# Moving two of the second block's four gate weight pieces behind the transposed gradient tiles in one DMA queue

## The chip, the cores and the metric

The kernel runs on one core of a Trainium2 chip. A core has a matrix engine (TensorE; PE for its matmuls and PEld for its weight loads in the profile), VectorE (DVE), ScalarE (ACT), GpSimd (POOL) and SyncE (SP), whose queue sends most of the DMAs. The metric is the device time of one execution in microseconds (us); lower is better.

## The reference, cut to what matters

The forward pass normalises x row by row and adds three terms; the kernel returns the output and the gradients of nine of its inputs.

```
xn   = layernorm(x)                                  # x: 2048 rows x 1024
out  = x + A(xn, k, v, shift_k, ssm_k, ssm_D)        # a long convolution branch
         + B(xn, W_gate, W_up, W_down)               # the gated branch:
gate = xn @ W_gate ; up = xn @ W_up                  # 1024 x 3584 each
h    = (gate if gate > 0 else 0) * up
B    = h @ W_down                                    # 3584 x 1024
# backward: gradients of out with respect to x, k, v, shift_k, ssm_k, ssm_D, W_gate, W_up, W_down
```

The backward pass of the gated branch needs `grad_out @ W_down.T`, the gradient of h.

## The kernel before, in words

Everything is bf16 with sums in float32. The change lies in the first phase, `hidden` (line 1221). It works in 14 blocks `n`: two halves of the rows (8 tiles of 128 rows each), and in each half seven blocks of 512 columns of the hidden dimension. For every row tile `s` of a block it makes three products of eight matmuls each (`gemm8`, line 1150): the gate, `ps_g`, from the transposed activation tile `xnT` and the gate weights `wg`; the up product, `ps_u`, from `xnT` and `wu`; and the gradient row, `ps_h`, from the transposed gradient tile `goT` and the transposed down weights `wdT`. Each of the three weight blocks comes in four pieces of 256 KB, piece q serving matmuls 2q and 2q+1 of a product. `col_block` (line 1136) sends the four pieces of the gate or up weights, `row_piece_T` (line 1168) one piece of the down weights, as a transposing DMA.

The first block (`n == 0`, `ahead` in the code) is special, since the layer norm runs at the same time. Activation tiles 0 to 5 are transposed on the matrix engine; tiles 6 and 7 by transposing DMAs in `flip_xn` (line 1185) that wait until VectorE has scaled these rows. Gradient tiles are transposed by DMA in `load_T` (line 1174). Its matmuls run in this order: rows 0 to 3 gate and up; gradient rows 0 and 1; gate and up of rows 4 and 5; gradient rows 2 to 5; gate and up of rows 6 and 7; gradient rows 6 and 7. Then the second block begins: gate of rows 0 and 1, up of rows 0 and 1, gradient rows 0 and 1, and so on.

The weights of the second block are loaded during the first: the gate weights by `load_gate` (line 1244) after gradient rows 0 and 1, into buffers that are spare; the up weights into the buffers of the first block's gate weights, and the down weights into those of its up weights, as these become free.

All these loads go through SP's queue, which issues in order: an entry that waits holds back all behind it. A scheduler sets the order of the entries from priorities that grow through the program; `issue_after(x)` keeps what is written under it behind `x`, and `pin` keeps an instruction in the written order. A DMA on SP's queue carries one of eight semaphores in turn and waits until the DMA eight places before it is complete. In this stretch the queue holds: four gate pieces of the second block, gradient tiles 4 and 5, activation tiles 6 and 7, gradient tiles 6 and 7, four up pieces, four down pieces. POOL's queue sends the stores of this block: `h_d`, `ug_d`, and the normalised rows `xn_d`.

Of the kernel before, what the change touches and what calls it, by code (L numbers as in the profile page):

```python
# [17 lines left out]
P = 128  # L18
# [30 lines left out]
class ABranch:  # L49
# [47 lines left out]
    def load(self, out, in_):  # L97
        self.pri.now()
        ins = self.nc.sync.dma_start(out=out, in_=in_)
        if self.pin:  # L100
            self.tc.keep_in_program_order(ins)
        else:
            self.pri.pin(ins)
# [776 lines left out]
class LnMlp:  # L880
# [252 lines left out]
            st0 += n  # L1133
            yield

    def col_block(self, W, fb, name, s, amid={}, ahead=None):

        out = []
        for q in range(self.DT // 2):
            if q in amid:  # L1140
                amid[q]()
            t = self.w_tile(name, 4 * s + q)
            first = ahead is not None and q == 0
            ins = (ahead if first else self.nc.sync).dma_start(
                out=t[:], in_=W[q * 256:(q + 1) * 256, fb * 512:(fb + 1) * 512].rearrange("(k p) f -> p k f", p=P))
            self.pri.pin(ins, always=first)
            out.append(t)
        return lambda kt: out[kt // 2][:, kt % 2, :]

    def gemm8(self, ps, xT, w, mid=None, after={}):  # L1150
# [22 lines left out]

    def load_T(self, src, st, name, slot, always=False):
        t = self.act_tile(name, slot)
        self.pri.pin(self.nc.sync.dma_start_transpose(out=t[:].rearrange("p (a b) -> p a b", b=P),
                                                      in_=src[st * P:(st + 1) * P, :]), always=always)
        return t

    def load_nat(self, src, st, name, slot):  # L1180
# [40 lines left out]
    def hidden(self, first, goT, load, ln, tables, Wg, Wu, Wd, g, xn_d, h_d, ug_d):  # L1221
# [6 lines left out]
        for n in range(N):  # L1228
            half, fb = divmod(n, self.FB)
            s0, cols, ahead = half * HS, slice(fb * 512, fb * 512 + 512), n == 0  # L1230
# [6 lines left out]
            wg, wu, wdt = w  # L1237
            wd = lambda kt, t=wdt: t[kt // 2][:, kt % 2, :]
            sg, su, sd = sets
            to = (spare, sg, su) if ahead else (sg, su, spare)  # L1240
            nb = (n + 1) % self.FB
            ru, nw, late = {}, [None, None, None], []

            def load_gate():
                if last:
                    self.slab_part(h_d, 0, "hs", self.hs, 4, sg)
                else:
                    nw[0] = self.col_block(Wg, nb, "wg", to[0])

# [4 lines left out]
            def load_down(q):  # L1254
                if last and q == 0:
                    self.slab_part(h_d, 0, "hs", self.hs, 0, spare)
                elif not last:
                    if q == 0:
                        nw[2] = []
                    nw[2].append(self.row_piece_T(Wd, nb, "wdT", to[2], q, n == 1))  # L1260
# [105 lines left out]
            def gate_up(sp):  # L1366
                end = sp == HS - 2
                if ahead and not end:
                    gate(sp)
                    yield from step(self.PACE[0])  # L1370

                    def turn():
                        flip(sp + 2)
                        with self.tc.issue_after(self.copied.ins):
                            chunk()
                    up(sp, None, {4: turn})
                    yield from step(self.PACE[1])
                    gate(sp + 1)
                    yield from step(self.PACE[0])
                    up(sp + 1)  # L1380
                    yield from step(self.PACE[1])
                    return
                rows = [(f, s) for f in (gate, up) for s in (sp, sp + 1)]
                for f, s in sorted(rows, key=lambda r: r[1]) if ahead else rows:
                    f(s)
                    yield from step(self.PACE[f is up])
                    if end and f is gate and s == sp + 1:
                        (load_up if ahead else load_gate)()
                if end and ahead:
                    for q in range(4):  # L1390
                        load_down(q)
                elif end:
                    load_up()
                if swap:
                    next_rows(sp)
# [8 lines left out]
            def last_rows(sp):  # L1404

                self.hold = self.busy = True
                for q in range(2):
                    load_down(sp // 2 + q)

                def run(f, s):  # L1410
                    f(s)
                    yield from step(self.PACE[f is up])
                yield from run(gate, sp)
                yield from run(gate, sp + 1)
                yield from run(up, sp)
                yield from run(gate, sp + 2)
                yield from run(gate, sp + 3)
                load_gate()
                yield from run(up, sp + 1)
                yield from grad_row(sp)  # L1420
                yield from run(up, sp + 2)
                yield from run(up, sp + 3)
                load_up()
                self.busy = swap and not last
                if n == 1:
                    chunk()
                if swap:
                    next_rows(sp)
                    next_rows(sp + 2)
                for s in range(sp + 1, HS):  # L1430
                    yield from grad_row(s)
                if swap:
                    next_grads(sp)
                    next_grads(sp + 2)
# [37 lines left out]
            def grad(sp):  # L1472
                for s in (sp, sp + 1):
                    at = 3 if sp == 0 else 0
                    yield from grad_row(s, {at: lambda: flip_ahead(sp)} if ahead and s == sp + 1 else {})
                if swap:
                    next_grads(sp)

            def chunk(steps=3):
                with self.tc.issue_after(self.ln_act.ins):  # L1480
                    for _ in range(steps):
                        next(ln)
# [7 lines left out]
            for sp in range(0, HS, 2):  # L1490
                self.pri.now()
                while len(gT) < min(sp + 4, HS):
                    with self.tc.issue_after(self.turned.ins if sp == 4 else self.copied.ins):
                        gT.append(self.load_T(g, len(gT), "goT", HS + len(gT)))
                if ahead or sp < HS - 4:
                    if not ahead:
                        load_down(sp // 2)
                        yield from gate_up(sp)
                        if n == 4 and sp == 2:
                            for k in filter(self.bare, range(HS)):  # L1500
                                xT[k] = self.load_T(xn_d, k, "xnT", k)
                        if sp:
                            self.hold = False
                        elif fb:
                            self.busy = False
                    if not ahead or sp != 4:
                        yield from grad(sp)
                    if ahead and sp == 2:
                        yield from grad(4)
                elif sp == HS - 4:  # L1510
                    yield from last_rows(sp)
                if ahead:
                    with self.tc.issue_after(self.stored.ins):
                        if sp == 0:
                            load_gate()
                if ahead and sp in (2, 6):
                    with self.tc.issue_after(self.put.ins):
                        for put in self.kept[0:4] if sp == 2 else self.kept[4:8]:
                            put()
                if ahead and sp == 6:  # L1520
                    with self.tc.issue_after(self.sent.ins):
                        load(6)
                if ahead and sp + 4 < HS:
                    yield from gate_up(sp + 4)
                if n == 1 and sp < 4:
                    with self.tc.issue_after(self.stored.ins):
                        for i in ((7,), (8, 9))[sp // 2]:
                            load(i)
                if n == 1 and sp != 4:
                    chunk()  # L1530
                if ahead and sp == 4:
                    with self.tc.issue_after(self.ln_act.ins), self.tc.issue_after(self.ln_dve.ins):
                        tables()
# [477 lines left out]
```

## Time and profile before

| | |
|---|---|
| median of 3 runs | 1848.75 us (1848.64 to 1848.85) |
| profiled execution | 1849.04 us |
| its span | 1847.3 us |
| matrix engine busy | 1827.6 us, 99% of the span |
| granted clock of the matrix engine | 1.00 |
| VectorE, ScalarE, GpSimd busy | 1118.2, 647.1, 34.9 us |
| first block | up to about 50.3 us |
| second block | 50.3 to about 92 us |

Times in the views are from the start of the span. A line such as `32.82 7.07 PE L1152 MATMUL ps_h<-wdT,goT ... x31` says when a group starts, how long it lasts, on which engine, from which line of the code, what it writes and reads, and how many instructions it merges; a bracket tells the idle time of the engine before it and what ended that. SPq is the queue of SP: its durations are those of issuing a DMA, not of the transfer. Some matmul records are missing from a trace, so a group of 32 can show 31.

### The profile page before, as it was taken

To read this page: it belongs to the slowest core of one execution; us is meant where nothing else is said; L and a number is where in the kernel's file an instruction comes from. 1 tells how busy PE (TensorE), PEld (TensorE's weight loads), DVE (VectorE), ACT (ScalarE), POOL (GpSimd) and SP (SyncE) were. 2 spreads that over 40 slices of the span, in tenths; PEclk is the share of its full clock that TensorE was granted. 3 is DMA by queue.
4 is the path that set the end of the run, shared out by engine and by line. 5 is a ranking of instruction groups with operands and counts; after the bars stand their busy time and mean duration, and the time that the engine had idled before them with its cause. 6 is when DMAs were issued, how large, how long until landed. Compare 5 with 4: busy or idle time off the path is not lost.

```text
span 1847.3 us, 32176 instructions
## 1 busy us (share of the span) xinstructions
PE 1827.6 (99%) x12970; PEld 846.9 (46%) x13182; DVE 1118.2 (61%) x1652; ACT 647.1 (35%) x1218; POOL 34.9 (2%) x72
## 2 busy tenths in 40 slices
PE   9999999999999999999999999999999999999999
PEld 4444444444444444444444444444444544444444
DVE  6656898698789758585685767721222222566652
ACT  6644544545444454544544455320000000111100
POOL 2200000000000000000000000000000000000000
PEclk9999999999999999999999999999999999999999
DMA  9997769969857866639566445389999767799973
GB/s 257 289 223 176 175 174 228 211 167 211 186 154 207 234 165 155 171 104 267 132 160 166 143 117 161 106 239 243 248 254 249 178 143 172 171 210 215 201 157 75
DMA packets 749989, 345.97 MB, mean 187 GB/s; under 512 B 581272, under 2 KB 718480, under 8 KB 749840
## 3 DMA queue, kind: packets, MB, share of 16 engines
q1 hardware_dynamic: 736048, 312.18, 71.5%
q10 hardware_dynamic: 9632, 17.04, 2.9%
q0 software_dynamic: 4160, 14.68, 2.3%
q8 instruction: 103, 1.69, 0.4%
q14 instruction: 46, 0.38, 0.1%
HBM read 143.79 MB, written 103.83 MB: 134 GB/s over the span
## 4 chain that ended last, share of the span: by engine, by line
PE 98%; issue 1%; DMA 0%; ACT 0%; SPq 0%; DVE 0%; ACTq 0%
PE ps_x L1860 21%; PE ps_w L1561 20%; PE ps_h L1152 10%; PE ps_u L1152 10%; PE ps_o L1728 10%; PE ps_g L1152 10%; PE ps_d L1561 9%; PE ps_c L83 4%; PE ps_d L1577 1%; PE ps_w L1577 1%; PE ps_r L1762 0%; DMA wg<-in_B_W_gate_dram 0%; DMA wu<-in_B_W_up_dram 0%; PE ps_u L1320 0%; ACT ln_j L965 0%
## 5 line engine op out<-in xcount | busy, mean ns | idle before, releaser
L1561 PE MATMUL ps_w<-ugs,xn_nat 128*128 128x512 bf16 x1675 | 375.2, 379 | 4.7 <-issue 2.9
L87 ACT CAST arena<-ps_c 128x512 bf16<-128x512 f32 x576 | 293.8, 611 | 103.0 <-PE ps_c L83 102.7
L1152 PEld LDWEIGHTS <-xnT 128*128 128x128 bf16 x1760 | 168.7, 98 | 205.2 <-issue 5.0
L1561 PEld LDWEIGHTS <-xn_nat 128*128 128x128 bf16 x1728 | 165.3, 98 | 200.8 <-issue 6.1
L343 DVE STREAM_TRANSPOSE arena<-arena 128x1024 f32<-128x1024 f32 x96 | 179.4, 1934 | 112.2 <-ACT arena L87 101.7
L1152 PE MATMUL ps_h<-wdT,goT 128*128 128x512 bf16 x873 | 201.9, 379 | 1.2
L1152 PE MATMUL ps_u<-wu,xnT 128*128 128x512 bf16 x861 | 201.3, 379 | 1.2
L1152 PE MATMUL ps_g<-wg,xnT 128*128 128x512 bf16 x848 | 199.4, 379 | 1.5
L1860 PE MATMUL ps_x<-wuT,guT 128*128 128x512 bf16 x878 | 197.5, 379 | 1.0
L1860 PE MATMUL ps_x<-wgT,ggT 128*128 128x512 bf16 x878 | 197.3, 379 | 0.9
L1878 ACT ACTIVATE w<-xn,m 128x512 f32<-128x512 bf16 x32 | 24.3, 806 | 479.9 <-DVE m L1871 366.6
L1728 PE MATMUL ps_o<-wd,hT 128*128 128x512 bf16 (+1 forms) x879 | 186.7, 372 | 0.9
L1561 PE MATMUL ps_d<-g_nat,hs 128*128 128x512 bf16 x743 | 166.5, 379 | 2.6 <-issue 1.9
L1860 PEld LDWEIGHTS <-guT 128*128 128x128 bf16 x896 | 87.7, 98 | 105.7
L1860 PEld LDWEIGHTS <-ggT 128*128 128x128 bf16 x896 | 87.7, 98 | 105.5
L1152 PEld LDWEIGHTS <-goT 128*128 128x128 bf16 x896 | 86.6, 98 | 104.3 <-issue 1.0
L1728 PEld LDWEIGHTS <-hT 128*128 128x128 bf16 x896 | 87.7, 98 | 99.9
L1449 ACT CAST gh<-ps_h 128x512 bf16<-128x512 f32 x112 | 66.2, 592 | 185.3 <-PE ps_h L1152 170.2
L1564 ACT CAST wi<-ps_w 128x512 bf16<-128x512 f32 x108 | 64.5, 597 | 187.6 <-PE ps_w L1561 149.1
L1720 DVE TENSOR_TENSOR ya<-ya,xe 128x1024 bf16<-128x1024 bf16 x16 | 11.1, 692 | 182.4 <-DMA xe<-xn_d 182.4
L91 DVE TENSOR_TENSOR t<-arena 128x2048 bf16<-128x2048 bf16 x96 | 114.0, 1220 | 0.4
L1561 PEld LDWEIGHTS <-hs 128*128 128x128 bf16 x768 | 73.3, 98 | 88.3 <-issue 1.8
(152 smaller groups left out, 1424.5 us busy)
## 6 DMA issues: line engine op xcount, KB each, us to landing
ugs<-ug_d SPq DMA_DIRECT2D x112, 256.0 KB
ug_d<-ru SPq DMA_DIRECT2D x104, 256.0 KB
wu<-in_B_W_up_dram SPq DMA_DIRECT2D x56, 256.0 KB
hs<-h_d SPq DMA_DIRECT2D x56, 256.0 KB
out_dram<-wi SPq DMA_DIRECT2D x56, 256.0 KB
wg<-in_B_W_gate_dram SPq DMA_DIRECT2D x55, 256.0 KB
h_d<-ht SPq DMA_DIRECT2D x104, 128.0 KB
gt<-in_grad_out_dram SPq DMA_DIRECT2D x32, 256.0 KB
```

The costliest lines, as they stand in the source:

```text
L83: self.pri.pin(self.nc.tensor.matmul(out, lhsT=lhsT, rhs=rhs, start=start, stop=stop))
L87: self.pri.pin(self.nc.scalar.copy(out=out, in_=in_))
L91: self.pri.pin(self.nc.vector.tensor_tensor(out=out, in0=in0, in1=in1, op=op))
L343: self.pri.pin(self.nc.vector.transpose(out=df[:, c0:c0 + 32, :], in_=sf[:, c0:c0 + 32, :]))
L1152: self.pri.pin(self.nc.tensor.matmul(ps[:], lhsT=xT[:, kt * P:(kt + 1) * P], rhs=w(kt), start=(kt == 0), stop=(kt == self.DT - 1)), always ...
L1449: self.pri.pin(nc.scalar.copy(out=gh[:], in_=ps[:]), **kept)
L1561: self.pri.pin(self.nc.tensor.matmul(ps[:], lhsT=lhsT(st), rhs=rhs(st), start=(st == 0), stop=(st == self.ST - 1)))
L1564: self.pri.pin(self.nc.scalar.copy(out=out, in_=ps[:]))
L1577: self.pri.pin(self.nc.tensor.matmul(ps[i][:], lhsT=lhsT(i, st), rhs=rhs(i, st), start=(st == 0), stop=(st == self.ST - 1)))
L1728: nc.tensor.matmul(ps, lhsT=hT[:, kt, :], rhs=self.wd[:, kt, oc], start=(kt == 0), stop=(kt == self.FT - 1))
L1860: nc.tensor.matmul(ps, lhsT=T[:, kt, :], rhs=W[:, kt, oc], start=(i == 0), stop=(i == n - 1))
L1878: nc.scalar.activation(out=w[:, oc], in_=xn[:, oc], func=ACT.Identity, scale=m[:, 7:8], bias=m[:, 6:7])
```

## The change

`load_gate` is called twice in the first block. The first call, where the only one was, sends pieces 0 and 1. The second, when the loop reaches `sp == 4` and the last gradient tiles have been sent, sends pieces 2 and 3 behind the last of them (`self.loaded`, which `load_T` now keeps). In SP's queue the order becomes: gate pieces 0 and 1, gradient tiles 4 and 5, activation tiles 6 and 7, gradient tiles 6 and 7, gate pieces 2 and 3, four up pieces, four down pieces. The order of every other instruction on every engine is the same as before; the semaphores that the moved entries carry, and those that wait for them, change with the place.

```
     def col_block(self, W, fb, name, s, amid={}, ahead=None, part=range(4), out=None):
-        out = []
-        for q in range(self.DT // 2):
+        out = [] if out is None else out
+        for q in part:
...
             out.append(t)
+        self.pieces = out
         return lambda kt: out[kt // 2][:, kt % 2, :]
...
     def load_T(self, src, st, name, slot, always=False):
         t = self.act_tile(name, slot)
-        self.pri.pin(self.nc.sync.dma_start_transpose(...), always=always)
+        self.loaded = self.nc.sync.dma_start_transpose(...)
+        self.pri.pin(self.loaded, always=always)
         return t
...
             def load_gate():
                 if last:
                     self.slab_part(h_d, 0, "hs", self.hs, 4, sg)
+                elif ahead and nw[0] is None:
+                    nw[0] = self.col_block(Wg, nb, "wg", to[0], part=range(2))
+                    nw.append(self.pieces)
+                elif ahead:
+                    self.col_block(Wg, nb, "wg", to[0], part=range(2, 4), out=nw.pop())
                 else:
                     nw[0] = self.col_block(Wg, nb, "wg", to[0])
...
                         gT.append(self.load_T(g, len(gT), "goT", HS + len(gT)))
+                if ahead and sp == 4:
+                    with self.tc.issue_after(self.loaded.ins):
+                        load_gate()
```

More of the change, by code (lines that the diff above doesn't have):

```diff
@@ L1134, in layer_norm, with col_block @@
             yield
-    def col_block(self, W, fb, name, s, amid={}, ahead=None):
-        out = []
-        for q in range(self.DT // 2):
+    def col_block(self, W, fb, name, s, amid={}, ahead=None, part=range(4), out=None):
+        out = [] if out is None else out
+        for q in part:
             if q in amid:
@@ L1175, in load_T @@
         t = self.act_tile(name, slot)
-        self.pri.pin(self.nc.sync.dma_start_transpose(out=t[:].rearrange("p (a b) -> p a b", b=P),
-                                                      in_=src[st * P:(st + 1) * P, :]), always=always)
+        self.loaded = self.nc.sync.dma_start_transpose(out=t[:].rearrange("p (a b) -> p a b", b=P),
+                                                       in_=src[st * P:(st + 1) * P, :])
+        self.pri.pin(self.loaded, always=always)
         return t
```

## The prediction

> **What bounds the kernel now.** I read the first page from the top, then who waited for whom on the matrix engine, then the timeline of its matmuls, of its weight loads and of SP's queue around the change, 24 to 62 us. The page's first row and the chain that ended last:
>
> ```profile
> PE 1827.6 (99%) x12970; PEld 846.9 (46%) x13182; DVE 1118.2 (61%) x1652; ACT 647.1 (35%) x1218; POOL 34.9 (2%) x72
> ...
> PE 98%; issue 1%; DMA 0%; ACT 0%; SPq 0%; DVE 0%; ACTq 0%
> ```
>
> The kernel is one string of matmuls: a transfer costs time only where a matmul or its weight load stands and waits for it. So I ask the waits of the weight loads over the whole span which transfers do that. Columns: who, for what, us in total, times, longest.
>
> ```profile
> PEld L83 <- issue: 47.9, 113, 0.4
> PEld L1561 <- issue: 7.8, 36, 0.4
> PEld L1152 <- issue: 6.0, 29, 0.2
> ...
> PEld L1152 <- DMA xnT<-ln_x: 0.5, 1, 0.5
> ...
> PEld L1577 <- DMA xn_nat<-xn_d: 0.2, 1, 0.2
> PEld L1152 <- DMA hs<-h_d: 0.2, 1, 0.2
> PEld L1561 <- DMA gks<-gks: 0.2, 1, 0.2
> ```
>
> "issue" is time that no wait explains. The longest wait for a transfer is `xnT<-ln_x`: the two transposes of activation tiles 6 and 7 that `flip_xn` sends, and these stand in SP's queue behind the four gate pieces. The timeline of SP's queue (start, duration of the issue, what):
>
> ```profile
> 25.80 0.58 SPq L237 DMA_DIRECT2D sk_b<-in_A_shift_k_dram  x1
> 26.43 2.61 SPq L1144 DMA_DIRECT2D wg<-in_B_W_gate_dram  x4
> 29.09 5.46 SPq L1176 DMA_TRANSPOSE goT<-in_grad_out_dram  x2
> 34.66 2.79 SPq L1188 DMA_TRANSPOSE xnT<-ln_x  x2
> 37.51 3.65 SPq L1176 DMA_TRANSPOSE goT<-in_grad_out_dram  x2
> 43.98 2.45 SPq L1144 DMA_DIRECT2D wu<-in_B_W_up_dram  x4
> 46.52 8.30 SPq L1170 DMA_TRANSPOSE wdT<-in_B_W_down_dram  x4
> ```
>
> And the matrix engine there, first its matmuls, then its weight loads:
>
> ```profile
> 32.82 7.07 PE L1152 MATMUL ps_h<-wdT,goT 128*128 128x512 bf16 x31
> 39.89 1.90 PE L1152 MATMUL ps_g<-wg,xnT 128*128 128x512 bf16 x8
> ...
> 43.35 1.89 PE L1152 MATMUL ps_g<-wg,xnT 128*128 128x512 bf16 x8
> ...
> 46.81 3.62 PE L1152 MATMUL ps_h<-wdT,goT 128*128 128x512 bf16 x16
> 50.26 3.62 PE L1152 MATMUL ps_g<-wg,xnT 128*128 128x512 bf16 x16
> 53.71 3.62 PE L1152 MATMUL ps_u<-wu,xnT 128*128 128x512 bf16 x15
> 57.17 3.62 PE L1152 MATMUL ps_h<-wdT,goT 128*128 128x512 bf16 x16
> ```
>
> ```profile
> 39.88 6.59 PEld L1152 LDWEIGHTS <-xnT 128*128 128x128 bf16 x32 [0.49 <-DMA xnT<-ln_x]
> ```
>
> Sixteen matmuls take 50.26 - 46.81 = 3.45 us, 0.216 each. The 32 of gradient rows 2 to 5 (one record is missing) should take 6.90 from 32.82 and end at 39.72; gate row 6 starts at 39.89. So the matrix engine loses 0.17 us there, waiting for activation tile 6. The weight load itself is idle 0.49; between two loads it is idle 0.12 anyway (0.216 less 0.098, the mean of one), so it is 0.37 late, and as the loads run about 0.2 ahead of the matmuls, 0.17 comes through. The same comes out twice.
>
> **The change part by part.** The only instructions that change place are two of SP's DMAs: before, four gate pieces, gradient tiles 4 and 5, activation tiles 6 and 7, gradient tiles 6 and 7; after, two gate pieces, the same six transposes, two gate pieces, then the up pieces as before. No engine's work changes. Completion times below are the trace's records of the queues' semaphores, which no view prints.
>
> *What is taken from ahead of the transposes.* Pieces 2 and 3 were issued between 28.07 and 29.09, so each transpose can be issued 1.02 us sooner. They completed at 32.71 and 34.04, piece 1 at 32.00, so up to 2.04 us of the stream goes (two stores of POOL's share it). Gradient tile 4 was complete at 35.71, needed at 32.82 + 16 x 0.216 = 36.27; tile 5 at 37.45, needed at 38.0. They had 0.55 us to spare and get more: worth nothing. Activation tile 6 was issued at 34.66 and complete at 39.84, after the need. Its other condition is its normalisation: the DVE multiply for row 6 runs 32.65 to 33.14 (the timeline), so its issue can be as early as 33.14, and by SP's own issues falls at 34.66 - 1.02 = 33.64 at the latest if the earlier transposes take as long to issue. It then completes at 38.8 or sooner, where the weight load wants it at about 39.5. The stall goes whole: **-0.17 us**. Bounds: 0 if it stays late by all of it, -0.17 at the most, since the engine has no other wait here. What is late next is nothing: tile 7 needs the DVE multiply that ends at 35.71, so its issue moves only from 36.06 to about 35.8, SP standing meanwhile; it completed at 41.49 and is needed at 43.35, 1.9 us to spare. Behind that standing SP queue only gradient tiles 6 and 7 (complete at 43.79 and 44.97, needed at 46.81 and 48.5) and the gate pieces.
>
> *What the two pieces cost in the new place.* Gradient tile 7 was issued from 39.61 to 41.15; the pieces follow, at 0.5 us each, and are out by about 42.2, before the up pieces at 43.98, which wait for the matrix engine to release their buffers. SP has 2.8 us free there (41.16 to 43.98): its issues cost nothing, and if that room were gone, the up pieces would slip by at most those 1.0 us. The gate pieces go to the spare buffers and wait for none. With the 4.5 to 5.5 us from issue to completion that the four have now, they land at about 46 to 47.5; their matmuls are the fifth and seventh of row 0 of the second block, 50.26 + 0.86 = 51.1 and 51.6. They have 3.6 us or more to spare: nothing. Their semaphore waits on the matrix engine only change in number, already met.
>
> *What is now queued behind them.* The 512 KB run later by the same amount that the transposes run sooner; POOL's four stores of normalised rows (issued 42.09 to 43.70, complete at 46.1 to 49.4), the up and the down pieces come after. Spare time now, completion against need: up pieces 49.79 to 52.24 against 53.71 to 55.0, least 2.8; down pieces 53.69, 55.26, 55.95, 56.99 against 57.17, 57.6, 58.0, 58.47, the least 1.48 for the last. If the engines stay busy throughout, the delay is 0, because the same bytes have passed by then; the worst is the full 2.04, which would stall the last down piece by 2.04 - 1.48 + 0.17 (the engine is now that much earlier) = 0.73. The DMA share over 36 to 52 us is 1.17, 1.24, 0.98 and 1.14 (windows of 4 us), so the nearer bound is 0; I take **0**, and keep 0.73 for the range.
>
> One thing speaks against the relief: POOL's stores mix with SP's transfers (one issued at 28.00 completed at 33.39, between gate pieces 2 and 3), so they could use the time that the pieces give up, and tile 6 would gain only part of it. But POOL issues just two stores of 128 KB between 29.4 and 36.6, at 31.37 and 34.54, so there is little to use it. The Trainium skill, DMA: Bandwidth & Descriptors, section Queues, rings and completion order, states the mixing as a rule: each DMA engine takes turns between its queue rows, packet by packet. By that rule alone, with POOL's row always full, the sum would be near 0 instead of -0.17; the trace agrees with the turns and not with the full row. It is part of the first rival's chance.
>
> *Sum.* -0.17 + 0 + 0. Later stages follow shifted: no other transfer holds the matrix engine longer than 0.2 us in the three rows above, and the orders are the same. The profiled execution took 1849.04 us (span 1847.3 and 1.7 around it), 0.29 over the median of the runs, 1848.75; so 1849.04 would be 1848.87, and the median 1848.75 - 0.17 = **1848.6**.
>
> **The rivals.**
>
> *No gain.* Tile 6 stays late because its issue is not held by the gate pieces but by something else: the queue's room (gradient tile 5's issue takes 3.36 us, against 1.24 for the quickest transposes), POOL's stores, or the DVE. Against: the DVE is done 1.5 us before the issue, and 0.37 us sooner suffices. Time 1848.75.
>
> *A new wait: slower.* The late gate pieces push the down pieces, and the first gradient row of the second block waits for the last of them at 58.47 - 0.17. It decides from a delay of 1.31 us on. Price up to 0.73; with the gain kept the sum is +0.56, so 1849.3. For: that piece has the least spare time in the stage, and the DMA share dips to 0.98 at 44 to 48. Against: the delay must survive 10 us of a busy queue, in which any idle moment before lets it vanish.
>
> *The order brings more.* The transposes sooner also free POOL's stores and the DVE chain. No matmul waits for these now, so at most the other waits of up to 0.2 us go: 1848.2.
>
> **How the numbers follow.** The forecast has 0.73, no gain 0.11, the new wait 0.09, more 0.03; 0.04 is for something the trace of before does not show. Of these only the last can leave 0.2% (3.7 us, about what a measurement of this kernel can tell from no change): slower by that 0.03, faster 0.01, the rest 0.96. The range holds the forecast, no gain and the new wait, with the spread of the runs (0.1 either way) at both ends and the low end at the third rival: 1848.2 to 1849.4. No case of weight has another sign by the bound of 0.2%.
>
> **What would show it.** Right: the 0.49 us wait of the weight load for `xnT<-ln_x` at 39.9 gone; gate row 6 starting 6.90 us after the gradient rows; SP's queue with two gate pieces at 26.4 and two at about 40.5 to 42; no wait of the matrix engine for `wg`, `wu` or `wdT` between 50 and 60. Wrong: that wait still there (no gain), or a wait for `wdT` near 58 (new wait). The forecast fails altogether if a stall of several us stands anywhere else in the string of matmuls.

## The result, and the profile after

| | before | after |
|---|---|---|
| median, measured side by side (11 executions each) | 1848.93 us (1848.64 to 1850.42) | 1853.55 us (1849.66 to 1856.57) |
| ratio of the times | | 1.0021, 95% interval 1.0012 to 1.0031 |
| profiled execution (span) | 1849.04 (1847.3) | 1851.31 (1849.5) |

The change makes the kernel slower in this measurement. The prediction had 1848.6 with a range up to 1849.4, and gave "slower by over 0.2%" 0.03. The changed kernel's times are far apart, and that is part of the result: one execution is below 1850, four lie between 1851.3 and 1851.9, and six at 1853.5 or more. In just these six the granted clock of the whole span is 0.999 or 0.998 and not 1.0.

The page's first row has the same work on every engine as before, so only waits can make the difference (of the matrix engine's matmuls no record is missing here, and some were before):

```profile
PE 1843.3 (100%) x13182; PEld 847.7 (46%) x13182; DVE 1118.4 (60%) x1652; ACT 647.3 (35%) x1218; POOL 35.0 (2%) x72
```

The rest shows the step that was meant, and a new wait behind it. First SP's queue in the changed kernel (start, duration of the issue, what):

```profile
33.08 3.81 SPq L1190 DMA_TRANSPOSE xnT<-ln_x  x2
36.94 3.19 SPq L1177 DMA_TRANSPOSE goT<-in_grad_out_dram  x2
40.17 1.19 SPq L1144 DMA_DIRECT2D wg<-in_B_W_gate_dram  x2
43.72 3.57 SPq L1144 DMA_DIRECT2D wu<-in_B_W_up_dram  x4
47.38 8.48 SPq L1171 DMA_TRANSPOSE wdT<-in_B_W_down_dram  x4
```

The activation tiles are issued 1.58 us sooner than the 34.66 of before, the two late gate pieces stand where they were expected. Then the matrix engine's timeline in the same kernel; a bracket tells the idle time before a group and what ended it:

```profile
32.73 7.07 PE L1153 MATMUL ps_h<-wdT,goT 128*128 128x512 bf16 x32
39.64 1.89 PE L1153 MATMUL ps_g<-wg,xnT 128*128 128x512 bf16 x8
...
50.00 3.62 PE L1153 MATMUL ps_g<-wg,xnT 128*128 128x512 bf16 x16
53.45 3.62 PE L1153 MATMUL ps_u<-wu,xnT 128*128 128x512 bf16 x16
56.90 1.46 PE L1153 MATMUL ps_h<-wdT,goT 128*128 128x512 bf16 x6
59.86 2.32 PE L1153 MATMUL ps_h<-wdT,goT 128*128 128x512 bf16 x10 [1.50 <-DMA wdT<-in_B_W_down_dram]
62.01 3.62 PE L1153 MATMUL ps_g<-wg,xnT 128*128 128x512 bf16 x16
```

Gate row 6 now starts 39.64 - 32.73 = 6.91 us after the gradient rows (before: 7.07), so the wait for activation tile 6 is gone. But the first gradient row of the second block, one group of 16 before, is broken after its sixth matmul: the seventh waits for the last down piece. By the distance of the weight loads, 1.88 us against 0.216, that costs 1.66 us. Of the waits of the matrix engine's matmuls in the changed kernel, longest first, these two did not exist before (us in total, times, longest):

```profile
PE ps_h L1153 <- DMA wdT<-in_B_W_down_dram: 1.5, 1, 1.5
...
PE ps_u L1153 <- DMA wu<-in_B_W_up_dram: 0.3, 1, 0.3
```

I read the second as an echo of the first. A load of rows for the layer norm stands in SP's queue right behind the down pieces; it landed at 65.02 instead of 60.84 (completions here and below are the trace's semaphore records, which no view prints), and ScalarE, which works in order, stood for it:

```profile
62.21 0.59 ACT L1456 CAST gh<-ps_h 128x512 bf16<-128x512 f32 x1 [1.14 <-PE ps_h L1153]
65.04 1.06 ACT L965 ACTIVATE ln_j<-ln_x 128x1024 bf16<-128x1024 bf16 x1 [2.24 <-DMA ln_x<-in_A_q_dram]
```

The stores behind it, and with them SP's queue, were 2.4 to 4.4 us late from 68 us on (the up pieces of a later block are issued at 136.35 instead of 132.69), until at 141 us two of these up pieces came late and cost the matrix engine 0.88 us. No other profile below has that loss, so the link rests on this one chain.

The whole difference of the two profiles adds up. The first weight load of `gemm8` (gate of row 2; the rows ahead of it have code of their own) starts at 13.93 us before and at 13.85 after, which is start-up and no part of the change: -0.08. The wait for tile 6: -0.18. The wait for the down piece: +1.66. The echo: +0.88. Sum +2.28; measured 1851.31 - 1849.04 = 2.27. The same sum holds for the other profiles below within 0.2 us: time = 1834.9 + start of that weight load + what the waits behind it cost. For a profile of the kernel before with no such wait (e5_before below) it gives 1834.9 + 13.53 = 1848.4; its time was 1848.46. With the starts seen in the profiles, 13.5 to 14.3, an execution without waits takes 1848.4 to 1849.2, and one at 1850.0 or more has lost 0.8 us or more somewhere.

So the place and the kind of the rival "A new wait" are right, and its price is not: it had 0.73 us at most. What had to be found out was why a piece that was 1.48 us early came 1.66 us too late or more, and what the executions with the lower clock are.

### The profile page after: what moved, and what is told of

It is laid out like the page before. It is cut to its first block, busy times and chain, and to the rows that moved or that the text cites. A ratio compares the mean times of both kernels' runs of the same rounds, so it can differ in the third digit from the quotient of the medians.

```text
span 1849.5 us, 32388 instructions
## 1 busy us (share of the span) xinstructions
PE 1843.3 (100%) x13182; PEld 847.7 (46%) x13182; DVE 1118.4 (60%) x1652; ACT 647.3 (35%) x1218; POOL 35.0 (2%) x72
## 4 chain that ended last, share of the span: by engine, by line
PE 99%; DMA 1%; DVE 0%; issue 0%; DVEq 0%
PE ps_x L1870 21%; PE ps_w L1571 20%; PE ps_h L1153 10%; PE ps_g L1153 10%; PE ps_u L1153 10%; PE ps_o L1738 10%; PE ps_d L1571 9%; PE ps_c L83 4%; PE ps_d L1587 2%; PE ps_w L1587 1%; PE ps_r L1772 0%; DMA wdT<-in_B_W_down_dram 0%; DMA wu<-in_B_W_up_dram 0%; PE ps_g L1327 0%; PE ps_u L1327 0%; PE pst_x L1198 0%
## 5 line engine op out<-in xcount | busy, mean ns | idle before, releaser
L1571 PE MATMUL ps_w<-ugs,xn_nat 128*128 128x512 bf16 x1728 | 381.1, 379 | 0.0
L1730 DVE TENSOR_TENSOR ya<-ya,xe 128x1024 bf16<-128x1024 bf16 x16 | 11.1, 692 | 175.1 <-DMA xe<-xn_d 175.1
```

What stands on the lines that cost most here:

```text
L1571: self.pri.pin(self.nc.tensor.matmul(ps[:], lhsT=lhsT(st), rhs=rhs(st), start=(st == 0), stop=(st == self.ST - 1)))
```

## The experiments

### First round: is it the bytes, or the place?

Two theories. A: while SP stands for VectorE (34 to 37 us), the DMA engines have too little to do, and the pieces that could have filled that time come later. B: whatever is put behind tile 6 delays the up and down pieces by its bytes, 512 KB. The first run is the changed kernel again, the second and third put pieces 2 and 3 in other places, the fourth leaves them out: it uses pieces 0 and 1 twice, so the gate product of the second block is computed with half of its weights (it also ties the third block's gate load, which is issued at 83 us, to a store; not shown in the cut).

```
e2_fill   between activation tiles 6 and 7 (the call behind the gradient tiles is taken out, here and in the two below):
+                    if len(xT) == 7:
+                        with self.tc.issue_after(self.turned.ins):
+                            load_gate()
e3_mid    behind activation tile 7, ahead of gradient tiles 6 and 7:
+                if ahead and sp == 4:
+                    with self.tc.issue_after(self.turned.ins):
+                        load_gate()
e4_none   pieces 2 and 3 not loaded:
+                    nw[0] = lambda kt, t=self.pieces: t[kt // 2 % 2][:, kt % 2, :]
```

Expected of the changed kernel again:

> The changed kernel once more, for its spread and for a second profile. Both theories: median 1851 to 1856 us against 1848.9 of the kernel before, executions spread over several us, and in the profile again a wait of about 1.5 us of the matrix engine for the down weights near 58 us. If the granted clock of some executions is under 1.00, these are the longest ones.

Of the pieces between the activation tiles:

> The two late gate pieces are sent between activation tile 6 and activation tile 7, where SP's queue of the changed kernel stands waiting for VectorE (33 to 35.7 us). Theory A (the DMA engines run dry while SP stands, and the lost transfer time is missing afterwards): the dip at 34 to 38 us is gone, no wait for the down weights at 58, and tile 6 is still in time, 1848.6 us within 0.3. Theory B (any order that puts these 512 KB after activation tile 6 delays the up and down pieces by their bytes): as the changed kernel, 1851 to 1855.

Of the pieces ahead of the gradient tiles:

> The two late gate pieces are sent behind activation tile 7 and ahead of gradient tiles 6 and 7. SP stands for VectorE as in the changed kernel and has nothing to send meanwhile. Theory A: the dip stays, so 1851 to 1855 us. Theory B: the same. If only the place behind the gradient tiles, next to the up pieces, does the harm: 1848.6.

Of the pieces left out:

> Gate pieces 2 and 3 of the second block are left out; its matmuls use pieces 0 and 1 twice, so that part of the computation is changed. 512 KB less in the stream. Both theories: no wait for the down weights near 58 us and no late activation tile 6, 1848.6 us within 0.4. If the reordering or the changed semaphores do the harm by themselves: 1851 or more.

Measured, 11 executions each, with the kernel before on the same chip at 1849.28:

| | median us | ratio (95%) | executions at 1850.0 or more | wait for `wdT` in the profile, loss |
|---|---|---|---|---|
| e1_again | 1850.70 | 1.0011 (1.0002 to 1.0019) | 10 of 11 | 1.16 |
| e2_fill | 1849.30 | 1.0001 (0.9992 to 1.0010) | 3 of 11 | 1.29 |
| e3_mid | 1849.02 | 1.0003 (0.9995 to 1.0012) | 3 of 11 | 1.57 |
| e4_none | 1848.90 | 0.9999 (0.9990 to 1.0008) | 1 of 11 | 0.98 |

Neither theory stands: both gave e3_mid 1851 or more, and e1_again, at 1850.70, is below their 1851 too. The third reading on record, that only the place behind the gradient tiles does harm, comes nearest by the medians, but the profiles speak against it: all four profiled executions have the wait for the last down piece, and all lie at 1850.15 to 1850.58, though most other executions of three of the kernels are near 1849. (In e1_again's profile 0.97 us more were lost at 22 us, to a gradient tile, ahead of everything that the change moves.) In all four the wait for tile 6 is gone, so that part does not depend on where behind the activation tile the pieces go. So the kernels seem to differ less in a delay than in how often one thing happens in an execution. The kernel before may have it too: 6 of its 33 executions on this chip are at 1850.0 or more. No profile was taken of such an execution of it; the single profile that the prediction was read from was one of the others.

### Second round: what decides whether the last down piece is late

Around the issue of that piece one other queue is active. POOL sends five stores of 256 KB in one go, the first as soon as VectorE has finished the last gradient row of the first block. POOL's timeline, first in the kernel before, then in the changed one:

```profile
54.69 0.69 POOL L1455 DMA_DIRECT2D ug_d<-ru  x1 [0.84 <-DVE k L172]
55.28 2.59 POOL L1001 DMA_DIRECT2D xn_d<-ln_x  x4
```

```profile
54.43 0.69 POOL L1462 DMA_DIRECT2D ug_d<-ru  x1 [0.84 <-DVE k L172]
55.02 2.60 POOL L1001 DMA_DIRECT2D xn_d<-ln_x  x4
```

In the kernel before, SP starts to issue the last down piece at 53.52, 1.17 us ahead of them; in the changed one at 54.38, 0.05 ahead. Theory C: the piece loses the DMA engines to these stores when it isn't issued clearly sooner. Theory D: the two extra entries make everything behind them late, whoever else stores. To tell them apart I moved POOL's stores and nothing else: twelve small iotas on POOL, into a tile that nobody reads, ahead of the first store. The order of every other engine stays. And, the other way round, I gave the kernel before the two entries without taking anything from ahead of tile 6 (pieces 2 and 3 are loaded a second time).

```
e7_hush    (and e9_hush_before, e10_hush, e12_hush_mid)
         hold(nc.gpsimd.iota(itNi[:], pattern=[[0, 1], [1, NB1]], base=0, channel_multiplier=0))
+        pad = con.tile([P, NB1], I32, name="pad")
+        [hold(nc.gpsimd.iota(pad[:], pattern=[[1, NB1]], base=k, channel_multiplier=0)) for k in range(12)]
e8_twice   all four pieces ahead of gradient tile 4 as before, and behind gradient tile 7:
+                    for q, t in enumerate(nw.pop()):
+                        if q > 1:
+                            self.nc.sync.dma_start(out=t[:], in_=Wg[q * 256:(q + 1) * 256, ...])
```

> The kernel before, unchanged, with a profile of its own on this chip. The times of its earlier executions lie in two groups, near 1848.9 and near 1850.3, and the one profile of it, 1849.04 us, shows no wait for the last down piece. If that piece decides between the groups, a profile at 1850.0 or more must show the matrix engine waiting 0.8 to 1.5 us for wdT near 59, and one at 1849.2 or less must show none. If the groups have another cause, a profile at 1850 shows no such wait.

> The changed kernel once more, unchanged, as the mark for the two below: 1850 to 1852, a wait of 1.0 to 1.7 us for the last down piece in its profile, and a few executions near 1855.

> The changed kernel, with twelve small iotas on POOL (into a tile that nobody reads) ahead of the last gradient store of the first block, so that POOL's five stores, which start at 54.4 us, start about 2 us later; every other engine's order is that of the changed kernel. Theory C (the last down piece loses the DMA engines to POOL's five stores, because they are issued before its own issue ends): the piece lands near 57.5, no wait for wdT of over 0.4 us, and 1848.4 to 1849.0, with the gain of the activation tile kept. Theory D (the two gate pieces make everything behind them on SP's queue late by their own issue, whoever else stores): the wait for wdT stays at 1.0 us or more and the time at 1850 to 1852.

> The kernel before, with gate pieces 2 and 3 of the second block sent where it sends them and a second time behind gradient tile 7 (so 512 KB more are moved): the 0.17 us wait for activation tile 6 stays, POOL's stores stay at 54.7, and the queue behind has the two entries more. Theory D: the entries alone do it, 1850.5 to 1852. Theory C by the earlier stores alone (the stores that come 0.25 us sooner when the wait for tile 6 is gone take the place of the down piece): 1848.8 to 1849.3, as before. Both together needed: in between, with some executions above 1850.

Measured; the kernel before on this chip has a median of 1849.69 and 10 of 33 executions at 1850.0 or more:

| | median us | ratio (95%) | executions at 1850.0 or more | profiled execution |
|---|---|---|---|---|
| e5_before | 1849.28 | 0.9998 (0.9988 to 1.0008) | 2 of 8 | 1848.46, no wait that cost time |
| e6_again | 1850.29 | 1.0002 (0.9994 to 1.0011) | 8 of 11 | 1854.40, waits 4.05 |
| e7_hush | 1848.79 | 0.9994 (0.9985 to 1.0003) | 0 of 11 | 1848.79, 0.11 |
| e8_twice | 1850.10 | 1.0002 (0.9993 to 1.0011) | 8 of 11 | 1854.15, waits 3.44 |

The profile of e5_before is of a short execution and has no wait for the piece, which is in keeping with that piece deciding, but can't tell what the long ones wait for. Theory C's numbers came for e7_hush. POOL's timeline there, with the stores 2 us later, and the matrix engine's, where the first gradient row of the second block is one group of 16 again:

```profile
51.67 4.49 POOL L209 IOTA pad<- 128x32 int32 x12
56.51 0.69 POOL L1462 DMA_DIRECT2D ug_d<-ru  x1 [0.35 <-issue]
```

```profile
53.35 3.62 PE L1153 MATMUL ps_u<-wu,xnT 128*128 128x512 bf16 x16
56.80 3.72 PE L1153 MATMUL ps_h<-wdT,goT 128*128 128x512 bf16 x16
60.36 3.62 PE L1153 MATMUL ps_g<-wg,xnT 128*128 128x512 bf16 x16
```

In e7_hush the piece was issued later than in the changed kernel, at 54.68 instead of 54.38, and still landed 3.48 us after that instead of 5.44. The DMA view says who had the engines: from 53 to 62 us the packets of the queue that moves POOL's stores took 42.6% of the time of the 16 DMA engines in the changed kernel, and 14.3% in e7_hush.

Theory D is not just wrong, though: e8_twice shows that two more entries do the harm without the earlier tile 6, with the stores where they were (54.82). That is the reading on record for "both together needed": the entries make the piece later, and the stores overtake it. It can't tell the entries from the 512 KB that it moves in addition, and the entries are not needed every time, since the profile of e4_none has the wait without them.

The two profiles at 1854 also show what the lower clock is. The matrix engine of e6_again, and the stretches around its wait (columns: us; busy PE, PEld, DVE, ACT, POOL; granted clock of PE; DMA share; GB/s):

```profile
56.74 1.03 PE L1153 MATMUL ps_h<-wdT,goT 128*128 128x512 bf16 x4
58.39 0.59 PE L1153 MATMUL ps_h<-wdT,goT 128*128 128x512 bf16 x2 [0.62 <-DMA wdT<-in_B_W_down_dram]
62.08 3.98 PE L1153 MATMUL ps_h<-wdT,goT 128*128 128x512 bf16 x10 [3.10 <-DMA wdT<-in_B_W_down_dram]
```

```profile
56.00:62.00 6.00, 2.36 (x11) 0.88 (x9) 4.22 (x15) 2.03 (x5) 1.63 (x4) 1.00 1.12 309
62.00:65.00 3.00, 2.92 (x7) 1.01 (x7) 0.69 (x1) 0.59 (x1) 0.00 (x0) 0.51 1.14 310
65.00:66.00 1.00, 1.00 (x5) 0.46 (x4) 0.00 (x0) 0.00 (x0) 0.00 (x0) 0.77 1.10 413
66.00:67.00 1.00, 1.00 (x7) 0.41 (x5) 0.29 (x1) 0.91 (x2) 0.00 (x0) 1.00 1.03 385
```

After a wait of 3.1 us the granted clock is 0.51 for some 3.4 us. The eight weight loads from 62.46 to 65.45 are 0.427 us apart instead of 0.216, 7 x 0.211 = 1.48 us more, and the one before them is 0.16 late: 1.64. The 64 weight loads from 53.07 on take 19.52 us, and 13.81 in a profile without a wait, so 5.71 are lost: 4.05 of waiting and, as the rest, 1.66 at half clock. By the sum above that is 1834.9 + 13.68 + 5.71 = 1854.3; measured 1854.40. In the changed kernel's own profile the wait was 1.5 us, and the clock stayed at 1.00.

The Trainium skill, TensorE: Matmul & The Clock Gate, section HAM oscillation — how this bites in real kernels, has this as a rule: a gap of the matrix engine over about 3.4 us lets its clock fall to half. The trace agrees on the half (0.51), but no gap here was that long: the fall came with waits of 3.1 and 3.3 us, and with 2.5 behind one of 1.4 (e11_all4 below), and not with 1.5.

What decides can be read from the clock records of the traces, which no view prints. In the three profiles with a half clock (e6_again, e8_twice, e11_all4) it lasts 3.41 us each time, and each time it begins 58.03 us after the first record of full clock. That is 17 times 3.41, so the clock seems to be set in windows of 3.41 us that run from there on, wherever the waits lie. Cut that way, the window ahead of each fall had the matrix engine idle for 3.08, 2.50 and 2.82 us; in the profiles that kept the full clock no window of this stretch has more than 1.50. So the same wait can cost the half clock or not, depending on how it falls across two windows: the 3.28 us of e8_twice were split into 0.77 and 2.50.

### Third round: the kernel before without the stores, and twice the dose

If theory C holds, the kernel before also loses its late executions when POOL's stores move, and four gate pieces behind the gradient tiles instead of two make every execution late.

```
e11_all4
-                    nw[0] = self.col_block(Wg, nb, "wg", to[0], part=range(2))
+                    nw[0] = self.col_block(Wg, nb, "wg", to[0], part=range(0))
...
-                    self.col_block(Wg, nb, "wg", to[0], part=range(2, 4), out=nw.pop())
+                    self.col_block(Wg, nb, "wg", to[0], part=range(4), out=nw.pop())
```

> The kernel before with the same twelve iotas on POOL, and nothing else changed. Theory C (the last down piece against POOL's five stores decides between the groups of times of the kernel before too): no wait for wdT in its profile, no execution above 1849.9, median 1848.7 to 1849.0, the wait of 0.17 us for activation tile 6 still there. If the groups of the kernel before have another cause, a third of its executions still lie above 1849.9.

> The changed kernel with the iotas once more, beside the kernel before with them. Theory C: no execution above 1849.9; below the run of the kernel before with iotas by the 0.17 us that the prediction gave to the activation tile, so 1848.5 to 1848.8, if that step held. Theory D (the two entries' own issue makes what is behind them late): at or above it.

> The changed kernel with all four gate pieces of the second block behind gradient tile 7, none ahead of tile 4: the double of the change. Theory C with the entries as what makes the down piece late: its issue about 1 us later than in the changed kernel, so it loses to POOL's stores in nearly every execution and by more; 1852 to 1856, most executions with a granted clock below 1. If the place of the stores alone decides and the entries do not count: 1850 to 1851, like the changed kernel.

> The gate pieces 2 and 3 behind activation tile 7 and ahead of gradient tiles 6, 7, with the iotas on POOL: no wait for tile 6, none for wdT; 1848.4 to 1848.7 by theory C, the lowest of the four. By theory D 1848.9 or more, as this order gave without the iotas (1849.02).

Measured; the kernel before on this chip 1849.28, 6 of 27 at 1850.0 or more:

| | median us | ratio (95%) | executions at 1850.0 or more | profiled execution |
|---|---|---|---|---|
| e9_hush_before | 1849.47 | 1.0001 (0.9992 to 1.0010) | 0 of 11 | 1849.00, no wait |
| e10_hush | 1848.68 | 0.9997 (0.9988 to 1.0006) | 0 of 11 | 1849.32, no wait |
| e11_all4 | 1855.41 | 1.0034 (1.0022 to 1.0047) | 5 of 5 | 1854.49, waits 4.25 |
| e12_hush_mid | 1848.89 | 0.9997 (0.9988 to 1.0006) | 0 of 11 | 1849.34, 0.41 for `goT` |

With the double dose all five executions lie between 1854.5 and 1856.7, each with a granted clock below 1. Its matrix engine waits for two down pieces:

```profile
59.38 0.59 PE L1153 MATMUL ps_h<-wdT,goT 128*128 128x512 bf16 x2 [1.38 <-DMA wdT<-in_B_W_down_dram]
62.51 3.73 PE L1153 MATMUL ps_h<-wdT,goT 128*128 128x512 bf16 x10 [2.54 <-DMA wdT<-in_B_W_down_dram]
```

With POOL's stores moved, no execution of any of the four kernels (44 in all) is above 1849.93. Without, it is 26 of 112 executions of the kernel before that are at 1850.0 or more, and 28 of 33 of the changed one. For the changed kernel, 0 of 22 against 28 of 33, that is theory C in its plainest form. For the kernel before it is less sure: 0 of 11 against 6 of 27 on the same chip can be chance (about 1 in 10), though two of its late executions, at 1853.27 and 1853.51, have the granted clock of 0.999 that the long waits leave. Four details missed. e9_hush_before has a median of 1849.47, where 1848.7 to 1849.0 was expected, and no wait for tile 6 in its profile, where 0.17 was. e10_hush lies 0.8 us below it instead of 0.17; tile 6 can't give that, the start-up differs by as much between executions, and both ratios hold 1. And e12_hush_mid was to be the lowest and isn't: with the gate pieces ahead of them, the gradient tiles come late, and its gradient row 7 waits (two weight loads are 0.82 us apart instead of 0.216, of which 0.41 reaches the string of matmuls):

```profile
48.68 1.90 PE L1153 MATMUL ps_h<-wdT,goT 128*128 128x512 bf16 x8 [0.23 <-DMA goT<-in_grad_out_dram]
```

The changed kernel with the iotas (1848.79 and 1848.68) has the lowest medians of all, but its ratios to the kernel before still hold 1: shown is that its late executions are gone, not that it is faster.

## Why the prediction was wrong, point by point

**The wait for activation tile 6.** Predicted to go whole, -0.17; it went in every kernel that sends the pieces later (-0.18 by the sum). But its worth was read from one execution. In the two other profiles of this order of the queue it cost nothing (in one of them the weight load is 0.02 late), and in e8_twice 0.13. The gain is there in some executions only, and start-up alone moves the time by more: the first weight load of `gemm8` starts between 13.5 and 14.3 us in the profiles.

**What the two pieces cost in the new place.** They were issued from 40.17 to 41.36 and landed at 45.8 and 46.5, needed at 50.9 and 51.3: right, nothing.

**"What is now queued behind them"** is the step that failed, in two terms. The delay was taken as 0 because the same bytes would have passed by then "if the engines stay busy throughout". In the changed kernel's profile the DMA share over 36 to 38 us is 0.75, against 1.28 before, so they were not busy throughout, and the last down piece was issued 10.7 to 11.5 us after the first up piece in the three profiles of the changed kernel, against 9.4 to 9.5 in three of the queue order of before. That the idle stretch is what made it late was not shown: e3_mid has a dip of the same kind (0.89) and was late in 3 of 11, and e8_twice has none (1.21) and was late. The profiles point to the entries behind the gradient tiles: none 9.4 to 9.5, two 10.7 to 11.5, four 12.2. They do not prove it, one execution each: with the iotas added, the changed kernel had 11.1 and 9.7, and e4_none, without entries there, 10.4.

The price was then bounded by 2.04 - 1.48 + 0.17 = 0.73, with 2.04 us as the most that the piece could come later. It was issued only 0.86 us later and landed 2.83 us later. The bound took it that a transfer which starts 1 us later also ends 1 us later. It doesn't: the iotas show that it matters which other queue starts to send in between. All profiles of the study, in the order of how long after POOL's first store SP begins to issue the last down piece:

| profile | issue of the piece less POOL's store, us | issue to landing, us | loss by waits for `wdT` |
|---|---|---|---|
| e9_hush_before | -3.4 | 3.41 | 0 |
| e10_hush | -3.2 | 3.62 | 0 |
| e7_hush | -1.8 | 3.48 | 0.11 |
| e12_hush_mid | -1.7 | 3.49 | 0 |
| e5_before | -1.3 | 3.33 | 0 |
| before | -1.2 | 3.47 | 0 |
| e2_fill | -0.3 | 5.34 | 1.29 |
| e4_none | -0.3 | 5.03 | 0.98 |
| e3_mid | -0.3 | 5.57 | 1.57 |
| after | -0.1 | 5.44 | 1.66 |
| e1_again | +0.1 | 4.75 | 1.16 |
| e8_twice | +0.7 | 6.51 | 3.44 + half clock |
| e6_again | +0.8 | 6.98 | 4.05 + half clock |
| e11_all4 | +1.5 | 6.51 | 4.25 + half clock |

Ahead by 1.2 us or more, the transfer takes 3.3 to 3.6 us; together with the stores, 4.8 to 7.0. No profile lies between -1.2 and -0.3. The 1.48 us to spare that the prediction found were measured on the good side of this step, and 0.86 us of delay, with stores that start 0.26 sooner, crosses it. The prediction had the rule for it in hand: the Trainium skill, DMA: Bandwidth & Descriptors, section Queues, rings and completion order, says that a DMA engine takes turns between its queue rows. By that rule, as an estimate, a transfer beside one other row that is always full takes twice as long; the traces are in keeping with that, 3.4 us against 4.8 to 7.0. I weighed it at 29 to 36 us, where POOL's queue is nearly empty, and not at 54 to 58, where POOL issues five stores.

**The sum.** It lacks two large terms: the wait (1.2 to 4.1 us in the three profiles of the changed kernel, where the sum has 0) and what follows from it: the half clock (1.66) after a long wait, or the loss at 141 us (0.88) in one of them.

**The chances.** "A new wait" had 0.09 and was the case. It was read from one execution in which the piece was on time. Three times are shown with the kernel before, 1848.64 to 1848.85, and the profiled one is 1849.04; later runs of it reach 1853.5. How much slower the changed kernel is depends on how many executions lose the race: by medians 4.6, 1.4 and 0.6 us in three measurements, and 1.0021 and 1.0011 of the first two are clear of 1, the third, 1.0002 (0.9994 to 1.0011), is not.

What stays open: why the last down piece is issued late at all. In the profiled execution of e4_none, where nothing stands behind the gradient tiles, it was late too (10.4 us after the first up piece); that execution was the only one of its 11 above 1850. And the spread below 1849.9 that is left in the kernels with the iotas was followed in the profiles only: there it is the start-up, 13.7 to 14.3 us.

## What to carry to other kernels

Time to spare of a transfer, read from one execution, is not a budget. Look which other queue begins to send between now and the new time: here a transfer that was moved past the start of a burst took up to twice as long, so 0.86 us of delay became 2.83. And the price of a wait of the matrix engine isn't linear either: with 2.5 us or more of it inside one window of 3.41 us it cost another 1.5 to 1.7 us of half clock, with 1.5 or less nothing more.

## What the runs showed of the hardware that was not expected

- The last down piece, 256 KB by a transposing DMA, took 3.3 to 3.6 us from issue to landing when it was issued 1.2 us or more ahead of five stores of POOL's queue, and 4.8 to 7.0 us beside them.
- The clock of the matrix engine halves inside a kernel that is otherwise 100% busy: after waits of 3.1 and 3.3 us, and after 1.4 and 2.5 close together, its weight loads were 0.427 us apart for about 3.4 us. After 1.5 us they were not. In the list of times such an execution is known by a granted clock of 0.999: as an estimate, 3.41 us at half clock are 0.0009 of the span. By the same estimate 0.998 is two such stretches; no profile shows one with two.
- Twelve iotas whose result nobody reads took the late executions of the changed kernel away: a delay of 2 us in the queue of POOL's stores, for which the matrix engine does not wait there.
